# A written-out order for two transformer layers: K of the first segment ahead of Q, and the whole instruction order planned anew

## The chip, the cores and the metric

The kernel runs on one core of one Trainium2 chip. The metric is the device time of that core in microseconds (us), from one execution; the number given for a kernel is the median of several executions. Beside the times there is one execution recorded by the hardware profiler, and every row, wait and duration below comes from that one.

The engines have short names in the profile: PE is TensorE's matrix multiplication and PEld its weight loading, DVE is VectorE, ACT is ScalarE, POOL is GpSimd, SP is SyncE, which here only issues DMAs.

## The reference

The computation is two identical layers over 2048 tokens of width 512. Each layer is an attention part with a memory (Infini-attention), then a gated feed-forward part, each behind a layer norm and with a residual.

```python
def _A_ref(x, wq, wk, wv, wo, beta):       # H = 32 heads of Dh = 16, N = 4 segments of L = 512
    q, k, v = heads(x @ wq), heads(x @ wk), heads(x @ wv)
    phi = lambda t: jnp.where(t > 0, t + 1.0, jnp.exp(t))
    for s in range(N):
        qs, ks, vs = q[:, :, s], k[:, :, s], v[:, :, s]
        p = softmax(qs @ ks.T * scale + causal_mask)
        a_dot = p @ vs
        pq = phi(qs)
        a_mem = (pq @ M) / (pq @ z + 1e-06)
        outs.append(g * a_mem + (1.0 - g) * a_dot)
        pk = phi(ks)
        M = M + pk.T @ vs
        z = z + pk.sum over tokens
    return concat(outs) @ wo

def _B_ref(x, w1, w3, w2):                 # F = 1376
    return (silu(x @ w1) * (x @ w3)) @ w2

for layer in range(2):
    x = x + _A_ref(layernorm(x), ...)
    x = x + _B_ref(layernorm(x), ...)
```

`heads`, `causal_mask` and the indexing stand for the reshapes that the reference writes out.

## The kernel before

The 2048 tokens are cut into the four segments, and the two layers make eight stages, numbered `g = 0..7` (`g = 4 * layer + s`). All weights stay in SBUF after they are loaded once. Tokens lie in `x_tok` as 16 tiles of 128 tokens.

A stage consists of these steps. `layer_norm` makes statistics (`bnst`, `bnag`), adds the epsilon (`lnve`), takes the power on POOL, normalises into `xn` and transposes into a `W` buffer: by TensorE in stages 0 and 1 (`turn`), by a DMA transpose from SP in the others. `project` makes Q, K and V as matmul groups named `q`, `k` and `v`, with evictions from PSUM named `evq`, `evk` and `evv`. In stages 0 and 1 each K group is also multiplied by a per-partition mask into `km` on DVE; later stages copy rows by DMA instead. `attention` makes the logits in bursts that the source marks with mode "R" (line 844), exponentiates them on ACT (line 853), masks diagonal blocks on POOL (line 866), and multiplies by V in bursts of mode "C" (`attend`, line 895). The result goes through a DMA transpose (line 910), `normalise` (`rd`, `rdg`, products on POOL or DVE), and a second DMA transpose named `oT` (line 955), whose output feeds `out_proj` (line 963). Stage 0 is handled in halves of 256 tokens. `phi` applies the feature map; `memory_update` sends phi(K) through DMA transposes (`pkT`, line 724) and multiplies it with V (the products `dacc`, line 735); `memory_read` makes the memory's part of the next stage (`mden`, the reciprocal `mrec`, `mnum`, `om`). `ffn` has the gate and up matmuls (`g` and `u`, line 994), a tanh on ACT, two products on DVE (`gp`, `hm`), and the down matmuls (`d`, line 1022).

None of this is executed in source order. Every instruction or burst is added to `Sched` with the data it reads and writes, an estimated duration, a priority and possibly a gate. `Sched.schedule` is a list scheduler that runs when the program is built. It goes through time with the estimates, and writes out one fixed order for each engine and for SP's queue. On the chip each engine follows its list, and only semaphores hold it back. Where an operation has two possible engines (an eviction on ACT or DVE, a product on POOL or DVE), the scheduler also chooses the engine.

How it picks the next instruction of an engine: each candidate has an earliest start `s` and a cautious start `w`; those whose `w` is within `LOOK` of the smallest are admitted, and the lowest priority number wins:

```python
w = max(tf, s + (R_SLACK if op.mode == "R" else SLACK[e]) + MARGIN.get(op.group[0], 0.0))
...
lim = max(smin, tf) + LOOK[e]
...
if pe_mode == "F" and s - op.avail_at < C_AGE:
    pr = 1e5 + pr
```

The last lines concern "C" bursts on TensorE: while TensorE is in ordinary matmuls ("F"), such a burst is put at the back until it has been available for `C_AGE` nanoseconds. `PRIO` adds to the priority of a named group in a stage (`("q", 3)` is the Q matmuls of stage 3), `GATE` moves the attention unit that such a group waits for, and `MARGIN` adds caution to a name in all stages. Priorities and margins never change what is computed.

The first loads are spread over two queues by `HEAD`: SP issues a token tile, then the Q weights, then token tile 2; ACT issues token tile 1, then token tile 3 and the K weights.

Of the kernel before, what the change touches and what calls it, by code (L numbers as in the profile page):

```python
# [29 lines left out]
PE_SWITCH = 100.0  # L30
PE_TAIL = 170.0
R_SLACK = 0.0
SLACK = {"pe": 60.0, "act": 90.0, "dve": 60.0, "pool": 0.0, "sp": 300.0}
LOOK = {"pe": 90.0, "act": 90.0, "dve": 10.0, "pool": 10.0, "sp": 40.0}
C_AGE = 1200.0
MARGIN = {"rd": 200.0}


class Pool:
# [328 lines left out]
def o_pe(ns):  # L368
# [4 lines left out]


PRIO = {
    ("", 0): 20, ("bnst", 3): -2.3, ("bnst", 7): -0.15, ("dacc", 4): -4, ("evX", 0): 1000.2, ("evk", 1): 1400,
    ("evk", 5): 1005, ("evq", 0): 300, ("evq", 7): 1751.7, ("evv", 0): 99.8, ("g", 3): -20, ("g", 5): 301.3,
    ("gp", 4): 998, ("hm", 6): 84.9, ("k", 4): -0.35, ("k", 5): 20.3, ("k", 7): -250, ("km", 2): -0.3,
    ("km", 4): 1000, ("ldwk", 0): -1.3, ("mblk", 2): 300, ("mrec", 3): -300, ("ph", 6): -0.6, ("phmin", 0): -100,
    ("phmin", 2): 0.05, ("q", 1): -300, ("q", 2): 0.6, ("q", 3): -550.05, ("q", 4): -0.3, ("q", 6): -999.7,  # L380
    ("rd", 0): 300, ("rdg", 1): -1, ("t", 7): -20, ("tanh", 5): -0.75, ("u", 1): -500, ("u", 4): -2002, ("u", 6): 780,
    ("v", 5): -0.15,
}
GATE = {
    ("bnst", 2): -1, ("bnst", 3): 1, ("bnst", 6): 3, ("ph", 0): -22, ("phexp", 0): -15, ("v", 1): -30, ("v", 6): 8,
    ("v", 7): 6,
}


def build(nc, A_x, A_wq, A_wk, A_wv, A_wo, A_beta, B_w1, B_w3, B_w2, out):  # L390
# [75 lines left out]
    def pe(fn, ns, mode="F", **k):  # L466
        return S.add([o_pe(ns)], fn, mode=mode, **k)
# [27 lines left out]
    for ee in range(2):  # L495
        dve(lambda e, ee=ee: e.tensor_reduce(cm[ee][:], bdm[:, ee::2, 0], axis=mybir.AxisListType.X, op=ALU.add), 4,
            reads=["bdm"], writes=["cm%d" % ee], prio=CP)
# [29 lines left out]
    pool(lambda e: e.memset(macc[:], 0.0), 544, writes=[("macc", 0), ("macc", 1)], prio=CP + 3)  # L527


    HEAD = (("sp", "q"), ("act", "3"), ("sp", "2"), ("act", "k"))  # L530

    xv = A_x[0].rearrange("(t p) d -> p t d", p=P)
    def ldx(q, i, prio):
# [116 lines left out]
    def project(s, g, X, first):  # L650
        z = Seg()
        z.q, z.k, z.km, z.va = new("W"), new("W"), new("km"), new("va")
        if first:
            jobs = []
            for hf in range(2):
                for A in (0, 2):
                    jobs += [("q", (A, A + 1), hf), ("k", (A, A + 1), hf)]
                jobs += [("v", (2 * hf,), 0), ("v", (2 * hf + 1,), 0)]
        else:
            jobs = [(k, (G,), None) for G in range(NCG) for k in ("q", "k")] + [("v", (i,), 0) for i in range(LT)]  # L660
        for n, (kind, Gs, hf) in enumerate(jobs):
            p0 = g - 0.95 + 0.05 * n
            gate = release(g, n)
            B = new("B")
            c0, c1 = (256 * hf, 256 * hf + 256) if hf is not None and kind != "v" else (0, 512)
            W = c1 - c0
            for a, G in enumerate(Gs):
                for cg in range(NCG):
                    st, sp_ = cg == 0, cg == NCG - 1
                    if kind == "v":  # L670
                        fn = lambda e, cg=cg, G=G, B=B, st=st, sp_=sp_: e.matmul(  # L671
                            bank(B), xa_r[X.slot][:, cg, 128 * G:128 * G + 128], wv_sb[:, cg, :], start=st, stop=sp_)
                        rd = [(X, G)]
                    else:
                        w = wq_sb if kind == "q" else wk_sb
                        fn = lambda e, cg=cg, G=G, B=B, st=st, sp_=sp_, w=w, a=a, W=W, c0=c0: e.matmul(  # L676
                            bank(B)[:, W * a:W * a + W], w[:, cg, 128 * G:128 * G + 128], xa_r[X.slot][:, cg, c0:c0 + W],
                            start=st, stop=sp_)
                        rd = [(X, i) for i in range(c0 // 128, c1 // 128)]
                    pe(fn, W / 2.4 + 2.5, mode="F", reads=rd + ["w" + kind], writes=[(B, 0)], bufs=[B, X],  # L680
                       prio=p0 + 0.001 * cg + 0.004 * a - 500, gates=[gate],
                       hold=[{"q": z.q, "k": z.k, "v": z.va}[kind]] + ([z.km] if kind == "k" and g <= 1 else []), name="%s%d.%d" % (kind, G, cg))
            if kind == "v":
                G = Gs[0]
                ev(lambda G=G: vheads(va_r[z.va.slot], G, 0, H)[:, :, 0:16], lambda B=B: bank(B).rearrange("p (h d) -> p h d", d=DH), 512,
                   reads=[(B, 0)], writes=[(z.va, G)], bufs=[B, z.va], prio=p0 - 100, name="evv")
                continue
            b = z.q if kind == "q" else z.k
            keys = [(G, h) for G in Gs for h in (range(2) if hf is None else (hf,))]
            part = lambda t, Gs=Gs, c0=c0, c1=c1: t[:, Gs[0]:Gs[-1] + 1, c0:c1]  # L690
            ev(lambda b=b, part=part: part(w_r[b.slot]), lambda B=B, m=len(Gs): bank(B).rearrange("p (g c) -> p g c", g=m), 512,
               reads=[(B, 0)], writes=[(b,) + x for x in keys], bufs=[B, b], prio=p0 - 100, name="ev" + kind)
            if kind == "k" and g <= 1:
                dve(lambda e, part=part: e.tensor_scalar(part(km_r[z.km.slot]), part(k_r[z.k.slot]), cm[1][:, 0:1], None,
                                                         op0=ALU.mult), 512, mode=1.5,
                    reads=[(z.k,) + x for x in keys] + ["cm1"], writes=[(z.km,) + x for x in keys], bufs=[z.k, z.km],
                    prio=p0 + 0.02 - (100 if g == 0 else 0), name="km")
            elif kind == "k" and Gs[0] == NCG - 1:
                for pg in range(4):
                    r = slice(32 * pg + 16, 32 * pg + 32)  # L700
                    S.add([("sp", 450.0, 2200.0)], lambda e, r=r: e.dma_start(km_r[z.km.slot][r], k_r[z.k.slot][r]), dmaq="sp",
                          mode="T", reads=[(z.k, a, h) for a in range(NCG) for h in range(2)], writes=[(z.km, pg, "p")],
                          bufs=[z.k, z.km], prio=g - 1 + 0.3, name="km", gates=[(g - 1, 0)])
        return z
# [116 lines left out]
    def attention(s, g, z, oms, parts):  # L821
        z.ot = new("W")
        cnt = 0
        for pi, part in enumerate(parts):
# [4 lines left out]
            for ui, (blocks, done, N) in enumerate(todo):  # L829
# [3 lines left out]
                for pgs in groups:  # L833
                    sb_ = [new("S") for _ in range(len(pgs) // 2)]

                    def sps(pg, pgs=pgs, sb_=sb_):
                        return pg if len(pgs) == 4 else 2 * sb_[0].slot + pg - pgs[0]

                    def lg(e, blocks=blocks, pgs=pgs, sps=sps, t1=t1):
                        o = None  # L840
                        for (G, ee, j, c, n) in blocks:
                            for pg in pgs:
                                kk, r = ((k_r[z.k.slot], 16), (km_r[z.km.slot], 32))[ee]
                                o = e.matmul(S4[:, sps(pg), c:c + n], kk[32 * pg:32 * pg + r, G, 128 * j:128 * j + 128],  # L844
                                             q_r[z.q.slot][32 * pg:32 * pg + r, G, 128 * t1 - n:128 * t1], start=True, stop=True,
                                             tile_position=(32 * pg, 0))
                        return o
                    u = pe(lg, N / 2.4 + 20, mode="R", reads=[(z.k, b[0], b[2] // 2) for b in blocks] +
                           [(z.km, b[0], b[2] // 2) if g <= 1 else (z.km, pg, "p") for b in blocks if b[1] for pg in pgs] +
                           [(z.q, b[0], h) for b in blocks for h in range((4 * t1 - b[4] // 32) // 8, t1 // 2)],  # L850
                           writes=[(x, 0) for x in sb_], bufs=sb_ + [z.k, z.km, z.q], prio=pr, gates=[last[-1]], name="R%d.%d" % (pi, ui))
                    last.append(u)
                    act(lambda e, N=N, ebuf=ebuf, pgs=pgs, sps=sps: e.activation(  # L853
                        e_r[ebuf.slot][:, pgs[0]:pgs[-1] + 1, 0:N], S4[:, sps(pgs[0]):sps(pgs[-1]) + 1, 0:N], ACT.Exp, scale=SCALE),
                        len(pgs) * N, reads=[(x, 0) for x in sb_], writes=[(ebuf, b[3], pgs[0]) for b in blocks],
                        bufs=sb_ + [ebuf], prio=pr, name="exp")
# [22 lines left out]
    def attend(s, g, z, pr, part, G, ees, where, xg, gates):  # L879
# [8 lines left out]
        def av(e):  # L888
# [8 lines left out]
            return o  # L897
        ebs = {id(where[k][0]): where[k][0] for k in keys}
        ncol = sum(where[k][2] for k in keys)
        pe(av, ncol / 2.4 + 10 * len(keys), mode="C", reads=[t for k in keys for t in where[k][3]] + [(z.va, j) for j in range(t1)],  # L900
           writes=[(X, 0) for X, xs, es in XS], bufs=[X for X, xs, es in XS] + [z.va] + list(ebs.values()),
           hold=[xs for X, xs, es in XS], prio=pr, gates=gates, name="C%d.%d" % (G, ees[0]))
        for X, xs, es in XS:
# [206 lines left out]
```

The softmax here doesn't subtract the row's maximum and nothing guards it: scores larger than these inputs give would overflow.

## Time and profile before

| | |
|---|---|
| median of 5 runs | 500.71 us (498.91 to 501.11) |
| the profiled execution's own time | 501.11 us |
| its span, first to last instruction | 499.4 us |
| PE busy | 473.6 us, 95% of the span |
| DVE busy | 403.6 us, 81% |
| ACT busy | 394.3 us, 79% |
| PEld busy | 215.1 us, 43% |
| POOL busy | 236.0 us, 47% |
| granted TensorE clock | 1.0 throughout |
| the busiest DMA queue, share of 16 engines | 31.2% |

The busy share is an average over the whole span. A stage can be bound by another engine than the one with the highest share, and because matmuls overlap, the end of each is modelled and a busy PE isn't necessarily at its peak. The span is 1.7 us shorter than the execution's own time, which includes what lies around the first and last instruction.

### The profile page before, as it was taken

How to read it: one execution, taken by the hardware profiler on the slowest of the kernel's cores; microseconds unless marked ns; L12 is line 12 of the kernel's file. 1: busy time of each engine (PE TensorE's matmuls, PEld its weight loads, DVE VectorE, ACT ScalarE, POOL GpSimd, SP SyncE). 2: the span in 40 equal slices, each digit the busy share in tenths (PEclk: the TensorE clock that was granted, in tenths of full speed). 3: DMA queues.
4: the chain of work that ended last, by engine and by line, in shares of the span. 5: the costliest groups of instructions: out<-in, count | busy, mean ns of one | idle time of the engine just before them, and what ended most of it. 6: DMA issues, size and time to landing. Idle time of an engine off the chain costs nothing.

```text
span 499.4 us, 10415 instructions
## 1 busy us (share of the span) xinstructions
PE 473.6 (95%) x4132; PEld 215.1 (43%) x4198; DVE 403.6 (81%) x802; ACT 394.3 (79%) x350; POOL 236.0 (47%) x350
## 2 busy tenths in 40 slices
PE   7989798999999999999999999999999999999997
PEld 4443345654444344334434444444344433444443
DVE  5899988997888689789967889889984797479572
ACT  3999899899989997799988999788987898731230
POOL 4857354575455555644544436445645563610000
PEclk9999999999999999999999999999999999999999
DMA  5947634322232241340441303522422224220201
GB/s 185 323 91 127 126 84 96 67 61 48 53 75 54 55 74 38 72 85 22 69 91 43 75 22 75 94 45 54 74 46 54 53 33 64 65 53 12 74 1 42
DMA packets 104160, 35.86 MB, mean 72 GB/s; under 512 B 96976, under 2 KB 102096, under 8 KB 104112
## 3 DMA queue, kind: packets, MB, share of 16 engines
q1 hardware_dynamic: 102432, 31.94, 31.2%
q0 software_dynamic: 720, 2.46, 1.8%
q10 hardware_dynamic: 960, 0.79, 0.5%
q8 instruction: 33, 0.54, 0.5%
q14 instruction: 15, 0.12, 0.1%
HBM read 8.43 MB, written 2.10 MB: 21 GB/s over the span
## 4 chain that ended last, share of the span: by engine, by line
PE 64%; DVE 21%; DMA 7%; issue 3%; ACT 3%; POOL 1%; SPq 1%
PE psall L994 24%; PE psall L1022 14%; PE psall L844 7%; PE psall L676 6%; PE psall L895 5%; PE psall L963 3%; DVE xn L618 3%; DVE ln L605 3%; PE psall L671 2%; DVE W L481 2%; DMA W<-W 2%; DVE x_tok L967 2%; ACT e L853 2%; DVE W L715 2%; DMA W<-og 2%
## 5 line engine op out<-in xcount | busy, mean ns | idle before, releaser
L853 ACT ACTIVATE e<-psall 128x2048 bf16<-128x2048 f32 (+1 forms) x180 | 301.1, 1702 | 39.3 <-PE psall L844 37.4
L866 POOL TENSOR_SCALAR_AFFINE_SELECT e<-e 128x512 bf16<-128x512 bf16 x256 | 163.8, 659 | 166.1 <-ACT e L853 164.2
L994 PE MATMUL psall<-W,w 128*128 128x512 bf16 (+3 forms) x768 | 166.0, 355 | 3.9 <-issue 1.0
L994 PEld LDWEIGHTS psall<-W,w 128*128 128x128 bf16 (+1 forms) x792 | 73.6, 100 | 76.0 <-issue 12.0
L1005 ACT ACTIVATE th<-psall 128x512 bf16<-128x512 f32 (+2 forms) x89 | 52.0, 594 | 40.7 <-PE psall L994 40.5
L1022 PE MATMUL psall<-w,h 128*128 128x512 bf16 (+1 forms) x335 | 82.6, 380 | 1.2 <-issue 0.5
L1007 DVE SCALAR_TENSOR_TENSOR gp<-th,psall 128x512 bf16<-128x512 bf16 (+2 forms) x89 | 59.3, 673 | 15.9 <-ACT th L1005 15.3
L1011 DVE SCALAR_TENSOR_TENSOR h<-gp,psall 128x512 bf16<-128x512 bf16 (+1 forms) x89 | 59.4, 673 | 9.0 <-PE psall L994 8.6
L1022 PEld LDWEIGHTS psall<-w,h 128*128 128x128 bf16 (+1 forms) x352 | 32.0, 98 | 37.6 <-issue 5.3
L605 DVE BATCH_NORM_STATS2 ln<-x_tok 128x6 f32<-128x512 bf16 x64 | 42.6, 681 | 2.1 <-DMA x_tok<-in_A_x_dram 1.6
L1027 DVE TENSOR_TENSOR x_tok<-psall,x_tok 128x512 bf16<-128x512 f32 x32 | 22.1, 689 | 26.8 <-PE psall L1022 26.8
L844 PE MATMUL psall<-W 16*128 16x256 bf16 (+3 forms) x544 | 41.3, 294 | 1.1 <-ACT e L853 0.7
L895 PE MATMUL psall<-e,va 128*32 128x256 bf16 (+3 forms) x1088 | 41.4, 293 | 0.9 <-DVE h L1011 0.4
L844 PE MATMUL psall<-W,km 32*128 32x256 bf16 (+3 forms) x544 | 40.8, 291 | 1.0 <-ACT e L853 1.0
L481 DVE CAST xs<-psall 128x512 bf16<-128x512 f32 x40 | 27.0, 685 | 13.8 <-PE psall L895 13.7
L676 PE MATMUL psall<-W,wk 128*128 128x512 bf16 (+1 forms) x139 | 34.1, 356 | 2.0 <-DVE xs L481 1.0
L618 DVE TENSOR_SCALAR xn<-x_tok,ln 128x512 bf16<-128x512 bf16 x64 | 33.7, 570 | 2.2 <-POOL ln L612 2.1
L676 PE MATMUL psall<-W,wq 128*128 128x512 bf16 (+1 forms) x137 | 33.2, 356 | 1.8 <-ACT W L480 0.9
L481 DVE CAST W<-psall 128x512 bf16<-128x512 f32 x45 | 30.2, 680 | 4.3 <-PE psall L676 4.1
L671 PE MATMUL psall<-wv,W 128*128 128x512 bf16 x121 | 32.2, 380 | 0.9 <-issue 0.8
L895 PEld LDWEIGHTS psall<-e,va 128*32 128x32 bf16 x1088 | 24.0, 96 | 19.4 <-issue 3.3
L963 PE MATMUL psall<-wo,W 128*128 128x512 bf16 x122 | 30.5, 380 | 1.6 <-DMA W<-og 0.8
(66 smaller groups left out, 423.6 us busy)
## 6 DMA issues: line engine op xcount, KB each, us to landing
w<-in_B_w_dram SPq DMA_DIRECT2D x4, 688.0 KB, 8.8
out_dram<-x_tok SPq DMA_DIRECT2D x16, 128.0 KB, 1.8
km<-W SPq DMA_DIRECT2D x24, 64.0 KB, 2.4
w<-in_B_w_dram POOLq DMA_DIRECT2D x3, 384.0 KB, 3.6
xg<-xs SPq DMA_TRANSPOSE x64, 2.4
x_tok<-in_A_x_dram POOLq DMA_DIRECT2D x2, 512.0 KB, 5.5
W<-xn SPq DMA_TRANSPOSE x56, 2.5
W<-og SPq DMA_TRANSPOSE x36, 2.4
```

Source lines behind the costliest of these rows:

```text
L481: return e.tensor_copy(dst(), src())
L605: dve(lambda e, i=i, tt=tt: e.bn_stats(ln_r[st.slot][:, i, 0:6], x_tok[:, tt, :]), 540, reads=[("x", tt)], writes=[(st, 0, i)], bufs=[st], ...
L676: fn = lambda e, cg=cg, G=G, B=B, st=st, sp_=sp_, w=w, a=a, W=W, c0=c0: e.matmul(bank(B)[:, W * a:W * a + W], w[:, cg, 128 * G:128 * G + 1 ...
L844: o = e.matmul(S4[:, sps(pg), c:c + n], kk[32 * pg:32 * pg + r, G, 128 * j:128 * j + 128], q_r[z.q.slot][32 * pg:32 * pg + r, G, 128 * t1 ...
L853: act(lambda e, N=N, ebuf=ebuf, pgs=pgs, sps=sps: e.activation(e_r[ebuf.slot][:, pgs[0]:pgs[-1] + 1, 0:N], S4[:, sps(pgs[0]):sps(pgs[-1]) ...
L866: pool(lambda e, ebuf=ebuf, c=c: e.affine_select(e_r[ebuf.slot][:, :, c:c + 128], e_r[ebuf.slot][:, :, c:c + 128], pattern=[[0, 4], [1, 128]],
L895: o = e.matmul(bank(X)[32 * pg:32 * pg + 32, base + W - n:base + W], va_r[z.va.slot][:, j, h:h + 32], e_r[eb.slot][:, pg, c:c + n], start= ...
L994: prev = pe(lambda e, i=i, cg=cg, ft=ft, B=B, w=w: e.matmul(bank(B)[0:width(ft), W * i:W * i + W], w[:, cg, 128 * ft:128 * ft + width(ft)] ...
L1005: act(lambda e, fw=fw, NW=NW, B=B, th=th: e.activation(th_r[th.slot][0:fw, 0:NW], bank(B)[0:fw, 0:NW], ACT.Tanh, scale=0.5), NW, reads=[(B ...
L1007: dve(lambda e, fw=fw, NW=NW, B=B, th=th, gp=gp: e.scalar_tensor_tensor(gp_r[gp.slot][0:fw, 0:NW], th_r[th.slot][0:fw, 0:NW], 1.0, bank(B) ...
L1011: dve(lambda e, fw=fw, NW=NW, B=B, gp=gps[fg], h=hs[fg]: e.scalar_tensor_tensor(h_r[h.slot][0:fw, 0:NW], gp_r[gp.slot][0:fw, 0:NW], 0.5, b ...
L1022: prev = pe(lambda e, ft=ft, fw=fw, B=B, h=h, c=c: e.matmul(bank(B), h_r[h.slot][0:fw, c:c + 128], w2_sb[0:fw, ft, :], start=(ft == 0), st ...
```

## The change

Three kinds of edit are made.

First, in stage 0 each pair of a Q group and a K group changes places in the list of jobs, so that the K group has the lower priority number. In `HEAD` the K weights go to SP's queue in the place of the Q weights, and the Q weights to ACT's.

Second, the planner's settings change: slacks, lookaheads, `C_AGE`, and `MARGIN`, which gets entries for the memory products (`dacc`), the epsilon of the layer norm (`lnve`), the reciprocal of the memory denominator (`mrec`), the transposes of the normalised attention (`oT`) and the product `rdg`. The estimates for a burst of logits and for a burst of attention times V get smaller by 16 ns, and by 7 ns for each block.

Third, the tables `PRIO` and `GATE` are replaced. Some entries stay as they were, some get other numbers, some go and others come.

No operation is added or removed in the source, and no shape or buffer changes.

```diff
-SLACK = {"pe": 60.0, "act": 90.0, "dve": 60.0, "pool": 0.0, "sp": 300.0}
-LOOK = {"pe": 90.0, "act": 90.0, "dve": 10.0, "pool": 10.0, "sp": 40.0}
-C_AGE = 1200.0
-MARGIN = {"rd": 200.0}
+SLACK = {"pe": 60.0, "act": 120.0, "dve": 60.0, "pool": 30.0, "sp": 300.0}
+LOOK = {"pe": 90.0, "act": 60.0, "dve": 10.0, "pool": 200.0, "sp": 60.0}
+C_AGE = 800.0
+MARGIN = {"dacc": 50.0, "lnve": 300.0, "mrec": 500.0, "oT": 3000.0, "rd": 200.0, "rdg": 100.0}
...
 PRIO = {
-    ("", 0): 20, ("bnst", 3): -2.3, ("bnst", 7): -0.15, ("dacc", 4): -4, ("evX", 0): 1000.2, ("evk", 1): 1400,
-    ("evk", 5): 1005, ("evq", 0): 300, ("evq", 7): 1751.7, ("evv", 0): 99.8, ("g", 3): -20, ("g", 5): 301.3,
-    ("gp", 4): 998, ("hm", 6): 84.9, ("k", 4): -0.35, ("k", 5): 20.3, ("k", 7): -250, ("km", 2): -0.3,
-    ("km", 4): 1000, ("ldwk", 0): -1.3, ("mblk", 2): 300, ("mrec", 3): -300, ("ph", 6): -0.6, ("phmin", 0): -100,
-    ("phmin", 2): 0.05, ("q", 1): -300, ("q", 2): 0.6, ("q", 3): -550.05, ("q", 4): -0.3, ("q", 6): -999.7,
-    ("rd", 0): 300, ("rdg", 1): -1, ("t", 7): -20, ("tanh", 5): -0.75, ("u", 1): -500, ("u", 4): -2002, ("u", 6): 780,
-    ("v", 5): -0.15,
+    ("bnag", 1): 503, ("bnag", 4): 0.6, ("bnag", 6): 100, ("bnst", 7): -1, ("evX", 0): 285, ("evX", 4): 100,
+    ("evk", 1): 1349, ("evk", 7): 18, ("evq", 7): 1751.7, ("g", 3): -20.85, ("gp", 4): 1298, ("gp", 6): 300.3,
+    ("hm", 3): 500, ("hm", 6): 86.9, ("k", 2): -1, ("k", 4): -0.35, ("k", 5): 20, ("km", 2): -500, ("km", 6): 1.95,
+    ("lnve", 3): -1000, ("mrec", 3): -305, ("phexp", 7): -99.7, ("q", 1): -20, ("q", 3): 0.15, ("q", 4): -0.3,
+    ("q", 6): -1299.55, ("rd", 0): 300, ("rd", 3): 50, ("rd", 4): 498.6, ("rdg", 5): 100, ("resA", 2): 300,
+    ("t", 7): -1000, ("u", 4): -2001.7, ("v", 1): 50, ("v", 2): 300, ("v", 5): -0.15, ("v", 6): -20,
 }
 GATE = {
-    ("bnst", 2): -1, ("bnst", 3): 1, ("bnst", 6): 3, ("ph", 0): -22, ("phexp", 0): -15, ("v", 1): -30, ("v", 6): 8,
-    ("v", 7): 6,
+    ("bnst", 2): -1, ("bnst", 3): 1, ("ph", 0): -23, ("phexp", 0): -4, ("v", 1): -40, ("v", 5): -9, ("v", 6): 8,
+    ("v", 7): 4,
 }
...
-    HEAD = (("sp", "q"), ("act", "3"), ("sp", "2"), ("act", "k"))
+    HEAD = (("sp", "k"), ("act", "3"), ("sp", "2"), ("act", "q"))
...
-                    jobs += [("q", (A, A + 1), hf), ("k", (A, A + 1), hf)]
+                    jobs += [("k", (A, A + 1), hf), ("q", (A, A + 1), hf)]
...
-                    u = pe(lg, N / 2.4 + 20, mode="R", reads=[(z.k, b[0], b[2] // 2) for b in blocks] +
+                    u = pe(lg, N / 2.4 + 4, mode="R", reads=[(z.k, b[0], b[2] // 2) for b in blocks] +
...
-        pe(av, ncol / 2.4 + 10 * len(keys), mode="C", reads=[t for k in keys for t in where[k][3]] + [(z.va, j) for j in range(t1)],
+        pe(av, ncol / 2.4 + 3 * len(keys), mode="C", reads=[t for k in keys for t in where[k][3]] + [(z.va, j) for j in range(t1)],
```

## Prediction

> **What bounds the kernel now.** I read four views in this order: busy times and slices, busy times by stage, the waits of TensorE, and the order of time at the start. The page's first two parts:
>
> ```profile
> PE 473.6 (95%) x4132; PEld 215.1 (43%) x4198; DVE 403.6 (81%) x802; ACT 394.3 (79%) x350; POOL 236.0 (47%) x350
> ...
> PE   7989798999999999999999999999999999999997
> ...
> DVE  5899988997888689789967889889984797479572
> ACT  3999899899989997799988999788987898731230
> ```
>
> PE has hardly a free slice after the first six. DVE and ACT are as full as PE in slices 2 to 8 only. The table by stage shows that early part more sharply, with PE, PEld, DVE, ACT and POOL in us, from the left:
>
> ```profile
> 20.00:30.00 10.00, 9.05 (x121) 4.51 (x120) 9.48 (x17) 9.79 (x12) 9.58 (x14) 1.00 0.92 175
> 40.00:50.00 10.00, 9.19 (x92) 3.22 (x92) 9.99 (x26) 9.88 (x11) 8.16 (x12) 1.00 0.75 119
> 50.00:60.00 10.00, 7.34 (x116) 3.73 (x119) 9.28 (x21) 8.07 (x10) 4.20 (x7) 1.00 0.75 145
> 250.00:300.00 50.00, 48.76 (x420) 20.33 (x427) 38.85 (x77) 44.34 (x37) 21.71 (x34) 1.00 0.27 56
> ```
>
> From 20 to 60 us DVE (9.28 to 9.99 of 10) and ACT bind and PE stands; from 100 on PE binds at over 96%. So an order can win in two places: the start up to 60 us, and PE's remaining gaps. Span less busy is 499.4 - 473.6 = 25.8 us. Of it about 6 us can't be planned away: 2.6 before 8.3 us (0.49 + 0.85 and the first 1.26), and 3.5 after the last matmul ends at 495.85. The waits of PE that end on data:
>
> ```profile
> PE psall L735 <- DMA W<-W: 2.7, 3, 1.4
> PE psall L844 <- ACT e L853: 1.7, 3, 1.0
> PE psall L676 <- DVE xs L481: 1.0, 1, 1.0
> PE psall L963 <- DMA W<-og: 0.8, 1, 0.8
> ```
>
> The first is the memory product waiting for phi(K)'s transposes; the columns are total us, times, longest. Listing in order of time every PE gap that ended on data, I get 5.5 us from 25 to 62 us and 7.6 us from 62 to 450. These 13 us are the most that a perfect order could take from PE's stalls; the rest of the 25.8 is short issue gaps of 0.2 us.
>
> [...] the chain of waits has 53 gate/up matmuls in 11.60 us, 219 ns each, while their row states 355 ns of one, so "95%" contains overlap. [...] PE stands 1.39 us at a memory product though feed-forward matmuls follow at once. So a wrongly placed instruction blocks all behind it. [...] the two 512 KB weight loads take 5.6 us from SP and 6.0 us from ACT. Exchanging their queues should then cost about 0.4 us of landing for Q and gain 0.4 for K.
>
> **The change part by part.**
>
> *K ahead of Q.* The start in order of time:
>
> ```profile
> 8.27 1.05 PE L676 MATMUL psall<-W,wq 128*128 128x256 bf16 x8 [0.85 <-ACT W L480]
> 9.15 1.04 PE L676 MATMUL psall<-W,wk 128*128 128x256 bf16 x8
> 10.23 0.60 ACT L480 ACTIVATE W<-psall 128x512 bf16<-128x512 f32 x1 [0.28 <-PE psall L676]
> 10.94 0.35 DVE L694 TENSOR_SCALAR km<-W,cm 128x512 bf16<-128x512 bf16 x1
> 11.64 0.26 PE L844 MATMUL psall<-W 16*128 16x128 bf16 x4
> 12.17 11.11 ACT L853 ACTIVATE e<-psall 128x1024 bf16<-128x1024 f32 x12
> ```
>
> The weights don't bind: issued at 1.27 and 1.25, they land at 6.9 and 7.3 (up to 7.7 from the end of the issue); PE starts at 8.27 when ACT's copy of the transposed tile ends. After the exchange both still beat 8.3 and 9.1. The chain to the first logits is K matmuls, eviction, mask on DVE (0.35), logits. With K first, its eviction takes the earlier ACT slot (9.35 to 9.95), and the mask, if the planner puts it there, fits where DVE waits 0.82 for the power on POOL; behind the two normalisations (10.29 to 11.03) it would gain nothing. The last condition becomes Q's eviction at 10.83 instead of the mask at 11.29: logits about 0.5 us sooner. The exponentials follow without a gap (11.11 us for 12), so some arrives; but ACT still has transposed tiles to copy until 12.28. I take **-0.3**, bounds -0.6 to +0.4 (Q late by the queue).
>
> *Memory products.* PE's three waits on line 735 are 1.39, 0.80 and 0.53 = 2.7 us. The margin itself moves the planned readiness by only 50 ns, 0.15 us for three; the rest depends on what the new order puts between. SP shows why they are late, with a V-result pair ahead and two xn transposes between:
>
> ```profile
> 78.92 2.57 SPq L910 DMA_TRANSPOSE xg<-xs  x2
> 81.54 3.88 SPq L724 DMA_TRANSPOSE W<-W  x3
> 85.52 2.52 SPq L634 DMA_TRANSPOSE W<-xn  x2
> ```
>
> Each takes 1.25 us of SP, so phi(K)'s four need at least 5 us plus the last one's landing of 2.5. Postponing oT lets pkT past it. I take half, **-1.4**; bounds -2.7 and +0.7, since behind a postponed product stand the matmuls queued on PE, the add to the memory (0.44), its mask (0.52) and the next stage's memory read.
>
> *The early stretch.* Entries for stage 0 and 1 of `evX`, `evq`, `evk`, `phmin`, `rd` and the gates reorder DVE, ACT and SP there. `ph` at -22 or -23 is ahead of all units either way, and costs nothing. `phexp` goes from no gate to the fifth unit; in the trace the first runs at 23.0, after many units, so it costs nothing while that cover stands, and one ACT slot of 1.08 us if not. `v` of stage 1 has no gate in both. The rest acts on 5.5 us of gaps where DVE is full: work can change places but not vanish. I take a fifth, **-1.0**; bounds -3 and +2.
>
> *C_AGE and the smaller estimates.* TensorE has 36 bursts of mode C, and in order of time 32 of them touch a burst of logits on one side, 4 stand alone between ordinary matmuls. With 800 instead of 1200 ns more would stand alone. A logits burst costs PE 0.33 us where its 512 columns should take 0.21 (estimate from the 219 ns per matmul above), so a change of mode costs about 0.1, with an issue gap 0.3. Ten more solitary bursts: **+0.3** (three at 0.1 each if the smaller estimates tighten others), bounds -1 and +3.
>
> *The wait that is added: oT, mrec, lnve, rdg.* These margins let other ready work go first. Behind oT on SP stand the xn, pkT and V-result transposes, which gain; behind its data stand the output projection, the residual, the next norm. The reciprocal (0.95 us, 6 times) and epsilon (0.21 us, 18 times) move by at most 0.5 and 0.3 us on a DVE that is about 82% busy from 100 to 450 us (285 of 350); PE has feed-forward matmuls to cover that. oT I take at 0 as well: in the last stage its transpose is issued at 446.95 and lands at about 449.4, and PE works through the previous stage's matmuls until 450.3. If that cover is gone it costs what rival B says.
>
> *Everything else in the tables* (stages 2 to 7) acts on gaps of about 4 us between 100 and 450 that are already single waits below 1 us: **0**, bounds -2 and +2.5.
>
> Sum: -0.3 - 1.4 - 1.0 + 0.3 = **-2.4 us**. Against the profiled execution's 501.1 that gives 498.7. That execution is the slowest of the five; the median is 0.4 lower, so I forecast **498.3** for the median.
>
> **Rivals.** *A, the order wins more:* the new plan takes over half of the 13 us of stalls, 7 of them, and the time is 493.7. For it: they are few waits, each with work behind it. Against: DVE is full in the early part. *B, oT becomes the new wait (slower):* a transpose held 3 us behind others. The place is the output projection, where PE already waited 0.78 us at 61.8 in stage 0: no cover there, two halves, 2 x 3 us at most. In stage 7 the cover is 450.3 - 449.4 = 0.9 us, so 2.1 us show. One bare half and the last stage are 3 + 2.1 = 5 us; without the gains, 501.1 + 5 - 0.4 = 505.5, with half of them 504. It decides once a transpose is held over 0.9 us in stage 7. Against it: with nothing else ready on SP the margin holds nothing back. *C, stalls only change places:* 500.7 less the 0.3 of the start, 500.4.
>
> **How the numbers follow.** Forecast 0.38, A 0.13, C 0.13, B and its weaker forms 0.36. A measurement can tell about 0.3%, 1.5 us, from no change. The forecast's own range of 496 to 500.5 gives 0.35 to faster and 0.03 to the same; A goes all to faster; C gives 0.11 to the same and 0.01 to each side; B gives 0.01 to the same and 0.35 to slower. So faster 0.49, same 0.15, slower 0.36. The range reaches from A's 493 to B's 505.5; forecast and C together have 496 to 501 as their own.
>
> **What would show it.** Right: first logits near 11.1 and first exponential before 12.0 us; the wait of line 735 for W<-W under 1.4 us; PE busier than 7.34 from 50 to 60 us; line 963 not waiting longer for og. Wrong: line 963 waiting over 2 us for W<-og, more than 10 solitary bursts of line 895, or PE busy over 476 us, which would mean that mode changes rather than waits decide.

## The result: 0.4% slower, and the profile after

The changed kernel takes 502.27 us (median of 43 runs), the kernel before 500.65 us (80 runs). The ratio is 1.0036 with a 95% interval of 1.0026 to 1.0045: 1.8 us slower on 500.6, where 2.4 us faster was forecast. Four of the 43 runs, at a mean clock of 0.976 to 0.980, took 509 to 512 us; they count in the median and not in the ratio. The changed kernel's own profiled execution took 501.91 us with a span of 500.2 us, 0.8 us more than before.

Its page, busy times and slices (the last row shown is the granted TensorE clock):

```profile
PE 474.4 (95%) x4133; PEld 215.6 (43%) x4198; DVE 406.7 (81%) x811; ACT 390.6 (78%) x343; POOL 232.6 (47%) x348
...
PE   8989799899999999899999998999999999999997
...
DVE  5999799987989799788986889889985597479572
ACT  3989799888989987889988998888987888840130
...
PEclk9999899999999999999999999999999999999999
```

PE's row leaves 500.2 - 474.4 = 25.8 us free, as before (499.4 - 473.6). Not all of that is idle time: both traces have about 65 matmul records fewer than the 4198 weight loads. The trace of a kernel that differs from before by three moves only (the memory products alone, below) has them all:

```profile
PE 481.9 (96%) x4198; PEld 214.9 (43%) x4198; DVE 403.3 (81%) x802; ACT 394.4 (79%) x350; POOL 235.7 (47%) x350
```

There PE is idle for 499.9 - 481.9 = 18.0 us. So, as an estimate from this trace, nearly 8 of the 25.8 us are missing records, and with them most of the "short issue gaps of 0.2 us" that the prediction counted.

The new thing is the fifth digit of the clock row: 8 where before there was a 9 everywhere. The table by stage (PE, PEld, DVE, ACT, POOL, then the clock) places it:

```profile
20.00:30.00 10.00, 8.28 (x118) 4.15 (x111) 9.96 (x19) 8.70 (x11) 9.31 (x14) 1.00 0.47 108
40.00:50.00 10.00, 9.17 (x95) 3.36 (x96) 9.76 (x26) 9.54 (x11) 8.67 (x13) 1.00 0.72 162
50.00:60.00 10.00, 7.63 (x69) 2.95 (x70) 7.06 (x17) 8.44 (x9) 4.27 (x8) 0.85 0.75 152
250.00:300.00 50.00, 48.54 (x419) 20.17 (x425) 39.41 (x77) 44.41 (x38) 22.73 (x35) 1.00 0.27 54
```

From 50 to 60 us PE looks busier than before (7.63 against 7.34) and does fewer matmuls (69 against 116): part of its time is at half clock (0.85 on average). Finer, the same table:

```profile
54.00:57.00 3.00, 0.96 (x7) 0.17 (x5) 2.13 (x5) 3.00 (x4) 0.00 (x0) 1.00 1.17 224
57.00:60.50 3.50, 3.33 (x8) 1.17 (x9) 1.43 (x3) 1.44 (x2) 2.52 (x5) 0.51 0.39 80
```

PE is nearly idle for 3 us (0.96 busy), and then its clock is at a half for 3.4 us (0.51 over the 3.5 shown). What it waited for and did, TensorE in order of time:

```profile
55.30 0.40 PE L843 MATMUL psall<-W 16*128 16x512 bf16 x4 [0.74 <-ACT e L852]
57.17 3.50 PE L962 MATMUL psall<-wo,W 128*128 128x512 bf16 x8 [1.47 <-DMA W<-og]
```

Eight output projections take 3.50 us; at the full clock eight such matmuls took 1.89 (in the run with the late load, below). The waits of TensorE on data (total us, times, longest; lines are one lower than before):

```profile
PE psall L843 <- ACT e L852: 2.0, 2, 1.2
PE psall L675 <- DVE W L480: 1.5, 2, 0.8
PE psall L962 <- DMA W<-og: 1.5, 1, 1.5
...
PE psall L993 <- DVE xs L480: 1.2, 1, 1.2
```

The row that led before, the memory product waiting for its transposes (2.7 us), is gone altogether. Others have come. From 62 to 113 us the two longest are

```profile
PE psall L993 <- DVE h L1010: 1.0, 1, 1.0
PE psall L894 <- DVE h L1010: 0.8, 1, 0.8
```

where before there were these two:

```profile
PE psall L735 <- DMA W<-W: 2.2, 2, 1.4
PE psall L963 <- DMA W<-og: 0.8, 1, 0.8
```

I summed the gaps of TensorE that ended on data, as the prediction did, after the first projections (9 us on):

| us | up to 62 | 62 to 113 | from 113 | sum |
|---|---|---|---|---|
| before | 5.5 | 2.2 | 5.5 | 13.1 |
| after | 4.7 | 2.0 | 6.6 | 13.3 |

The new order has moved the waits and not reduced them.

**The clock and the time.** Each run lists the mean clock granted to its core. Of the runs that enter the ratios, I put those with a mean of 0.999 or more beside the others:

| | at 0.999 or more | below |
|---|---|---|
| before (108 runs in four comparisons) | 500.49 (48) | 500.61 (60) |
| after (40 runs) | 501.52 (17) | 502.92 (23) |

The 108 runs of the kernel before were taken beside the experiments below. Over half of them are below full clock as well, and those runs are 0.1 us longer. In the changed kernel such runs are 1.4 us longer. At full clock it is still 1.0 us slower than the kernel before. So the loss is about 1.0 us of order plus 1.4 us in 23 of 40 runs, 0.8 on average. This sorts runs and is no experiment: it doesn't show whether the lower clock makes these runs longer or only comes with longer waits.

### The profile page after: what moved, and what is told of

It is laid out like the page before. It is cut to its first block, busy times and chain, and to the rows that moved or that the text cites. A ratio compares the mean times of both kernels' runs of the same rounds, so it can differ in the third digit from the quotient of the medians.

```text
span 500.2 us, 10435 instructions
## 1 busy us (share of the span) xinstructions
PE 474.4 (95%) x4133; PEld 215.6 (43%) x4198; DVE 406.7 (81%) x811; ACT 390.6 (78%) x343; POOL 232.6 (47%) x348
## 4 chain that ended last, share of the span: by engine, by line
PE 66%; DVE 20%; DMA 4%; ACT 4%; issue 3%; POOL 1%; SPq 1%
PE psall L993 24%; PE psall L1021 14%; PE psall L843 7%; PE psall L675 6%; PE psall L894 5%; PE psall L962 4%; ACT e L852 3%; PE psall L670 3%; DVE xn L617 2%; DVE W L480 2%; DVE ln L604 2%; DVE x_tok L966 2%; DMA xg<-xs 2%; DVE W L714 2%; DVE h L1010 2%
## 5 line engine op out<-in xcount | busy, mean ns | idle before, releaser
L993 PEld LDWEIGHTS psall<-W,w 128*128 128x128 bf16 (+1 forms) x792 | 73.6, 100 | 77.7 <-issue 11.5
L1004 ACT ACTIVATE th<-psall 128x512 bf16<-128x512 f32 (+2 forms) x89 | 51.6, 595 | 36.3 <-PE psall L993 36.3
L1010 DVE SCALAR_TENSOR_TENSOR h<-gp,psall 128x512 bf16<-128x512 bf16 (+2 forms) x89 | 59.7, 674 | 8.1 <-PE psall L993 7.2
L675 PE MATMUL psall<-W,wk 128*128 128x512 bf16 (+1 forms) x138 | 36.2, 356 | 2.5 <-DVE W L480 1.5
L480 DVE CAST W<-psall 128x512 bf16<-128x512 f32 x49 | 32.7, 679 | 7.1 <-PE psall L675 6.8
L675 PE MATMUL psall<-W,wq 128*128 128x512 bf16 (+1 forms) x138 | 36.5, 356 | 0.5 <-issue 0.5
L962 PE MATMUL psall<-wo,W 128*128 128x512 bf16 x122 | 31.6, 396 | 2.7 <-DMA W<-og 1.5
```

The source lines that it names most:

```text
L480: return e.tensor_copy(dst(), src())
L962: pe(lambda e, i=i, G=G, B=B: e.matmul(bank(B), ot_r[z.ot.slot][:, G, 128 * i:128 * i + 128], wo_sb[:, G, :], start=(G == 0), stop=(G == N ...
L993: prev = pe(lambda e, i=i, cg=cg, ft=ft, B=B, w=w: e.matmul(bank(B)[0:width(ft), W * i:W * i + W], w[:, cg, 128 * ft:128 * ft + width(ft)] ...
L1010: dve(lambda e, fw=fw, NW=NW, B=B, gp=gps[fg], h=hs[fg]: e.scalar_tensor_tensor(h_r[h.slot][0:fw, 0:NW], gp_r[gp.slot][0:fw, 0:NW], 0.5, b ...
```

## The experiments

Theory 1: TensorE starved in stage 0, and the half clock that follows, make the loss. Theory 2: the order of the later stages makes it. Theory 3: K first makes it.

**K first alone.** The kernel before with two lines changed; the planner lays out the rest anew.

```diff
-    HEAD = (("sp", "q"), ("act", "3"), ("sp", "2"), ("act", "k"))
+    HEAD = (("sp", "k"), ("act", "3"), ("sp", "2"), ("act", "q"))
-                    jobs += [("q", (A, A + 1), hf), ("k", (A, A + 1), hf)]
+                    jobs += [("k", (A, A + 1), hf), ("q", (A, A + 1), hf)]
```

> The kernel before with only the loads and the job order of stage 0 changed (K ahead of Q); settings and tables as before, so the planner lays out the rest again. Theory 1 (the loss comes from TensorE being starved at the output projection of stage 0, after which its clock is granted at half for 3.4 us): K first has no part in it, 500.4 within 1.5 of before, clock as before. Theory 2 (the new order loses in the stages 1 to 3, whatever the clock does): the tables were fitted to another start, so a new start with the old tables gives another order downstream: 501 to 505. Theory 3 (K first itself is the loss): 502, with the first logits no earlier than 11.6 us.

Measured: 506.92 us, ratio 1.0118 (1.0081 to 1.0155), worse than any theory had it. Five of its six runs were below full clock; the sixth, at full clock, took 501.66. In its profile (509.04 us) the order from 117 us on is that of before, and all milestones from 64 us on are late by 8 to 9 us, nearly constant: everything was lost before that. TensorE in order of time, and the table by stage:

```profile
46.01 1.03 PE L676 MATMUL psall<-W,wq 128*128 128x512 bf16 x2 [2.00 <-DVE xs L481]
...
59.19 4.42 PE L676 MATMUL psall<-W,wk 128*128 128x512 bf16 x11
```

```profile
44.00:46.00 2.00, 0.01 (x1) 0.00 (x0) 2.00 (x8) 1.79 (x2) 0.64 (x1) 0.99 0.42 63
46.00:48.00 2.00, 1.99 (x8) 0.47 (x9) 2.00 (x5) 0.38 (x1) 0.08 (x1) 0.50 0.58 194
54.00:56.00 2.00, 2.00 (x10) 0.39 (x8) 0.84 (x2) 1.38 (x2) 0.17 (x2) 0.50 0.56 122
62.00:64.00 2.00, 2.00 (x25) 1.03 (x23) 0.00 (x0) 0.95 (x2) 0.00 (x0) 0.75 0.55 118
```

One standstill of 2.0 us, behind DVE's copy that frees a PSUM bank, and then 17 us at half clock, from 45.9 to 63.0; the full clock comes back 3.8 us into the piece of eleven matmuls. DVE and ACT, which bind here otherwise, become idle (0.84 and 1.38 of 2 us from 54 on): PE is now the bound.

**The same order, the standstill filled.** One group of V is computed two more times at the place where TensorE stood, eight matmuls of no use.

```diff
+        self.again("v0.3", 1, ("v0.0", "v0.1", "v0.2"), 2)
```

> The kernel with K first and the old tables (506.9), in exactly its order, with one matmul group of V of stage 1 computed two more times ahead of the place where TensorE stood for 2.0 us at 44 us: eight matmuls more, 1.7 us of TensorE, the result is the same. If the loss of 6.6 us is the half clock that follows the standstill (17 us in its trace): 500.5 to 502.5, clock at 0.997 or more. If the standstill or the order itself is the loss: 506 to 508.

Measured: 501.88 us, ratio 1.0035 (1.0018 to 1.0051). Useless work made that kernel 5 us faster. Its runs at full clock have a median of 501.57 (13 runs), close to the one run of K first alone at full clock (501.66). So the 6.6 us of K first alone are about 5.3 of clock (506.9 - 501.6), and 1.1 of order that remains (501.6 - 500.5).

The remedy works in most runs and not in all. The profiled execution is one of the others (506.15 us): with the standstill filled, TensorE is at half clock from 31.3 to 45.0 us, in an earlier place. In the 3.4 us before that its row was busy for 2.58, with no single wait over 0.7 us:

```profile
27.89:31.30 3.41, 2.58 (x27) 0.96 (x24) 3.41 (x8) 3.41 (x4) 1.88 (x4) 1.00 0.37 79
```

**The gap of the changed kernel filled.** Eight matmuls of no use ahead of the first output projection of stage 0, in the order as it is.

```diff
+    S.fills.append(("o0", 0, 8, spare))
```

> The changed kernel in exactly its order, with eight extra matmuls (1.7 us of TensorE, on weights that lie there, into the PSUM bank that the first output projection of stage 0 overwrites) put ahead of that projection, where TensorE stood from about 55.6 to 57.2 us. Theory 1: the clock stays at 1.0 in every run, the spread at the top goes, and the median falls by 1 to 1.9 us, to 500.5 to 501.3. Theory 2: the clock may go up, but the median falls by under 0.5, to about 502. If the extra work delays the projection instead: up to 0.3 slower.

Measured: 503.79 us, ratio 1.0063 (1.0038 to 1.0088). A miss for theory 1: in the profile the clock holds at 57 us and the first output projections end 1.9 us sooner (58.8 against 60.7), but the half clock comes at 86.5 us instead, behind a wait of 1.0 us for DVE. Its four runs at full clock have 502.1, no less than the changed kernel's 501.5. Here filling one hole did not keep the clock; other holes remained.

**The late transpose of the changed kernel.** A 512 KB load of token tiles moves five places later in POOL's list; nothing else moves.

> The changed kernel with one move: the 512 KB load of the last four token tiles, which POOL issues at 51.7 us, comes five places later in POOL's list (after 57 us). Nothing else moves. If that load is what makes the transpose issued at 52.4 land only after 4.6 us: the landing takes 2.4 to 3, the output projection of stage 0 waits under 0.4 us instead of 1.5, no half clock follows it, and the median falls by 1 to 2 us, to 500.3 to 501.3. If the other transposes on SP make it late: within 0.5 us of 502.3.

Measured: 501.94 us, ratio 1.0021 (1.0010 to 1.0033). The cause was named rightly: the transpose, now issued at 52.1, lands after 2.9 us, and the eight projections start at 55.2 us and take 1.89, with no wait of their own. But TensorE's waits between 62 and 113 us:

```profile
PE psall L980 <- DMA W<-og: 1.9, 1, 1.9
PE psall L912 <- DVE h L1028: 1.2, 1, 1.2
```

The second half's projection now waits 1.9 us at 77 us, with 3.4 us at half clock right after. The gain is 0.3 us of the 1 to 2 expected, and the two intervals overlap.

**Q first again, and the margins back.** Each undoes one part of the changed kernel with the rest new.

> The changed kernel with Q ahead of K again in loads and jobs; new settings and tables stay. Theory 3: back to about 500.7. Theory 1: unchanged at 502.3 if the output projection of stage 0 still waits over 2 us in all, with a clock under 1.0 in part of the runs. Theory 2: 502 to 506, since the new tables then meet a start that they weren't made for.

> The changed kernel with MARGIN as before (only rd); everything else new. If the margin of oT is what makes the output projection late (the slower rival of the prediction): line 962 waits under 1 us for W<-og in stage 0 and the time is 500 to 501. Theory 1 without oT as its cause, and theory 2: 502 to 505, because the tables were made with the margins and the order downstream is again another one.

Measured: 508.92 us, ratio 1.0163 (1.0142 to 1.0185), and 507.81 us, 1.0137 (1.0116 to 1.0158). Both lie outside every range that I had given. Each undoing gives the planner an input for which the tables were not made, and the order changes everywhere; the largest data waits of the first are then 1.9 us at 340 us and 1.5 at 313, far from stage 0. Without the margins the output projections no longer wait for `W<-og` at all, and the kernel is slower still. The parts belong together: K first alone costs 1.2%, the new settings and tables alone 1.6%, both together 0.4%. What one part does within the whole, these two runs can't say.

**Starts and tails exchanged.** The settings are switched at a planner time, the tables by stage.

> Q first and the tables and settings of before for stage 0 until the planner's 55 us, then the new settings and tables. TensorE's list begins with the 196 entries of before and ends with exactly the last 1365 of 1961 entries of the changed kernel. If the loss sits in the start (the clock, stage 0): 500 to 501, as before. If it sits in the order of the later stages: 501.3 to 502.5.

> The reverse: K first with the new tables for stages 0 and 1 and the new settings until the planner's 120 us, then those of before. TensorE's list begins with the first 217 entries of the changed kernel and ends with the last 930 of before. If the loss sits in the start: 501.5 to 504, with a clock under 1.0 in some runs that goes with the time. If in the later order: 499.5 to 501. The middle part belongs to neither, so up to 3 us more are possible from there.

Measured: 503.09 us, ratio 1.0049 (1.0033 to 1.0066), and 507.62 us, 1.0125 (1.0106 to 1.0143). The first lies above both ranges and speaks for theory 2 only in part: the old start doesn't help, but all six runs were below full clock. The second is inconclusive: its middle belongs to neither kernel, and TensorE stands there for 2.0 us at 146 us, with 3.4 us at half clock right after.

What the later stages cost can be read from the traces of the other runs. Those of the changed kernel, of the filled gap and of its late load have the new order from stage 2 on; those of the kernel before, of K first, of K first filled and of the late load in the kernel before have the old one. From the first logits of stage 2 to the start of the last down projection the new order takes 382.7 to 383.1 us, the old one 381.5 to 382.3. That is about 1.0 more, close to the growth of the waits from 113 us on (5.5 to 6.6), and as much as the changed kernel loses at full clock. All these traces have full clock in that part.

**The memory products alone.** The order of before, three products (line 735) later in TensorE's list, past 12, 9 and 4 entries.

```diff
+        self.move('pe', [x for x in self.order['pe'] if x.name == 'dacc' and x.group[1] == 1][1], 12)
+        self.move('pe', [x for x in self.order['pe'] if x.name == 'dacc' and x.group[1] == 2][1], 9)
+        self.move('pe', [x for x in self.order['pe'] if x.name == 'dacc' and x.group[1] == 4][1], 4)
```

> The kernel before in its own order, with three memory products alone moved later in TensorE's list: that of 84.1 us past 12 matmuls, that of 93.4 past 9, that of 187.0 past 4, so that TensorE does these while the transposes land. It is the part of the change that the prediction valued at -1.4 (bounds -2.7 and +0.7), without anything else. If TensorE's waits add up to the time: the waits of line 735 for W<-W go from 2.7 to under 0.3 us and the median falls by 1.4 to 2.7, to 498 to 499.3. If the wait turns up at the next place that depends on the memory or on DVE: 500 to 501.

Measured: 502.36 us, ratio 1.0039 (1.0028 to 1.0050), at full clock 502.28 (11 runs). The wait for the transposes is gone, and the kernel is 1.8 us *slower*. From 75 to 100 us, TensorE's waits in this kernel:

```profile
PE psall L1025 <- DVE gp L1038: 0.9, 2, 0.6
PE psall L766 <- DVE h L1042: 0.7, 1, 0.7
PE psall L1025 <- DVE macc L772: 0.5, 1, 0.5
PE psall L1025 <- DVE h L1042: 0.5, 1, 0.5
```

They sum to 2.6 us, where before there were 2.2 for the transposes. And DVE's waits in the same stretch, first of this kernel, then of the kernel before:

```profile
DVE macc L772 <- PE psall L766: 2.9, 2, 1.6
```

```profile
DVE macc L741 <- PE psall L735: 1.1, 2, 0.7
```

DVE's list comes to the addition to the memory and stands there until the product is made. TensorE's list now has feed-forward matmuls ahead of the product, and they wait for what DVE makes behind that addition. So each list stands for the other. DVE pays more than TensorE's waits tell: these grew by 0.4 us, but the last of the three additions in this stretch starts at 95.6 us instead of 94.1, all of DVE's list behind it is later, and from the first logits of stage 1 to those of stage 2 it is 59.6 us instead of 58.3.

**Products and additions later.** The same, with the addition and its mask moved on DVE as well (past 4 and 2 entries at 84 us, 3 and 2 at 93).

> The kernel with the three products later (502.4), and in DVE's list the addition to the memory and its mask moved later with the products of 84 and 93 us: past four entries for the first, past three for the second, so that DVE makes feed-forward products while the memory products come. If the loss of 1.8 us is DVE's list standing at the addition while TensorE's list stands at DVE's products: DVE's waits for line 735's result between 75 and 100 us fall from 2.9 to under 1.2, and the time goes back to 499.5 to 501. If the loss comes from the later memory itself (the next stage's read): 502 to 503.5.

Measured: 501.81 us, ratio 1.0025 (1.0014 to 1.0035). That lies between the two ranges. DVE no longer waits for the product at all, as expected, but the median falls by only 0.5 us, and the two intervals overlap. In the profile stage 1 takes 58.9 us, between the two. Now TensorE waits 1.8 us for the later addition:

```profile
PE psall L1029 <- DVE macc L776: 1.8, 2, 1.3
```

**The late load in the kernel before, and both edits.**

> The kernel before in its own order, with the one 512 KB load of the last four token tiles moved five places later in POOL's list (from 53.2 us to about 60). In the changed kernel the same move shortened the landing but the standstill went from 57 to 77 us. If transposes that land after over 4 us cost the kernel before anything: the landing of the transpose issued at 57.5 falls from 4.2 to under 3, and 499.0 to 500. If standstills only change their place: 500.3 to 501.

> Both moves in the kernel before. If each is a gain by itself: 497.5 to 499. If waits only change their place: 500 to 501.

Measured: 500.76 us, ratio 0.9998 (0.9973 to 1.0023), and 503.05 us, 1.0053 (1.0033 to 1.0072). The first median is in the range of waits that only change their place, but the move did not do what it was for: in the profile the load, issued at 59.9 us, now falls on another transpose for the output projection. Issued at 58.5, that one lands after 5.9 us instead of 4.2, TensorE waits 3.9 us for it, and 6.8 us at half clock follow. That execution took 504.6 us. The second is slower than all its ranges. No version here beats the kernel before.

## Why the prediction was wrong

**The step that failed is the price of a wait.** "Memory products ... I take half, **-1.4**; bounds -2.7 and +0.7" and "The early stretch ... I take a fifth, **-1.0**" took a wait of TensorE as time that comes back when other work is put there. The mechanism came true: the waits of line 735 for the transposes went from 2.7 us to nothing. But from 62 to 113 us, where 2.2 of these had been, TensorE's waits on data are 2.0 us in the changed kernel, against 2.2 before. They now end on DVE's product `h` (1.0 and 0.8). The transposes had ended those waits last; that DVE was next, close behind, fits the profile of before, where DVE is full between two of them:

```profile
88.00:92.00 4.00, 3.87 (x64) 2.53 (x61) 4.00 (x8) 3.59 (x3) 2.02 (x3) 1.00 0.74 103
```

The same move alone, in the old order, measured +1.8 instead of -1.4, outside the bounds. I had named what stands behind the product ("the add to the memory (0.44), its mask (0.52)") and had not seen that DVE's list stands at that addition until the product comes (two waits in that run, 2.9 us in all), with work behind it that TensorE needs. In the changed kernel the planner placed DVE's work anew as well, so the 1.8 us can't be carried over to it; what is shown there is that the waits came back.

**How the sum came apart.** The forecast was -2.4 us, most of it in stages 0 and 1. At full clock the later stages account for about +1.0, the whole loss, so the gains of the first stages came to about nothing. The lower clock goes with another 0.8 on average, and had no term in the sum. Theory 1, which I held first after the result, falls in part: the clock goes with somewhat under half of the loss.

**K first** (-0.3): the chain got shorter as forecast, by about half a microsecond, and the gain did not come. In all seven traces with K first it is 2.8 us from the first projection to the first logits; in the seven with Q first it is 3.3 to 4.0. (The mask stands behind the two normalisations, where I had expected no gain.) But the first projection itself starts at 8.6 to 9.3 us with K first, against 8.2 to 8.8 with Q first, so the first logits start at 11.4 to 12.2 and 11.5 to 12.4 (11.50 in the changed kernel's trace, 11.64 before; I had said near 11.1). Why the first projection starts later is open. And the step left out what another order at the start does to the rest: with old tables a standstill of 2.0 us and 17 us at half clock.

**The early stretch** (-1.0): waits up to 62 us went from 5.5 to 4.7 us, but the time did not follow. From the first logits to those of stage 1 it is 43.4 to 43.8 us in four traces of the new start, 43.2 before and 43.2 to 44.2 in other traces of the old start. That PE is busier than 7.34 us from 50 to 60 us came true for a wrong reason: the half clock makes its work longer (3.50 us for eight projections instead of 1.89).

**oT, taken at 0.** This was the sharpest rival, and its place was right: the output projection of stage 0, bare, 0.78 us before and 1.47 after. Its size was not: the transpose was ready at 51.6 us and issued at 52.4 behind two xn transposes, held 0.8 us, not 3. What made it late was its landing after 4.6 us beside the 512 KB load, which the run with the late load shows (2.9 us there). In stage 7 the projection did not wait. The rival's sum is off by a little: 501.1 + 5 - 0.4 is 505.7. What the margins are worth within the new order is open, since without them the whole order is another one (507.8 us).

**C_AGE** (+0.3): no effect seen. 4 of 36 bursts stand alone between ordinary matmuls, before and after.

**Everything else** (0): about +1.0 in the stages from 2 on, the third of the memory products among them, and inside its bounds. Which entries make it wasn't tried.

**The rivals.** C, that stalls only change places, describes the waits (13.1 and 13.3 us) but not the time: none of the prediction's cases had TensorE's clock in it. I had read the clock row as 1.0 throughout and taken a short standstill as its own length.

What is left open: what starts the half clock in a given run, and why it then lasts 3.4 us in one and 17 in another; and most of the 1.8 us of the memory products, which moving the additions didn't clearly return.

## What to carry to other kernels

A wait on the engine that looks like the bound is only worth its length if nothing else would end it soon after (here 2.7 us of waits were taken away alone, and the kernel took 1.8 us more): look at which engine is next, where its list stands, and what it holds. In an order written out as one list for each engine, one instruction moved on one list must be followed on the lists that feed it and drain it. And where runs differ in the granted clock, compare runs at the same clock before explaining a fraction of a per cent by the order (the runs of the changed kernel at the two clocks are 1.4 us apart, 0.3%).

## What the runs showed of the hardware

In the profiles here TensorE's clock is granted at a half (0.50 in K first, 0.51 in the changed kernel) in stretches of 3.4 us (the changed kernel, from 57.0), 6.8 (the late load in the kernel before), 13.7 (K first filled, 31.3 to 45.0) and 17.1 us (K first, 45.9 to 63.0). What came before such a stretch differs: in K first a standstill of 2.0 us, after 4 us in which PE's row was full; in the changed kernel 0.96 us of work in 3; in K first filled 2.58 us in 3.41. And a full row did not end one: in K first PE is busy for 1.99 or 2.00 of every 2 us from 46 to 62 us, all at 0.50, and the full clock comes at 63.0, 3.8 us into the eleven matmuls. What starts and what ends such a stretch was not shown.

The price differs: runs below full clock are 0.1 us longer in the kernel before and 1.4 in the changed one, where eight projections at half clock took 3.50 us instead of 1.89. Why it differs was not shown.
